# Linear attention plus mixture of experts on one core: six q tiles turned through DRAM instead of on TensorE, and the routing table's lanes as Sign steps on ScalarE

## The chip, the cores and the metric

The kernel runs on one core of a Trainium2 chip. The metric is the device time of one execution in microseconds (us); the time before is the median of three runs, 826.5 us (826.42 to 826.99). A profile of one execution goes with it. The engines are TensorE (PE in the profile; PEld is its weight load), VectorE (DVE), ScalarE (ACT), GpSimd (POOL) and SyncE (SP, which only issues transfers here). Each works its own instructions off in order and waits for the others through semaphores.

## The reference

```python
xn = _layernorm(x)                                   # (2048, 512)
# attention: 32 heads of 16, phi(t) = where(t > 0, t + 1, exp(t)) + 1e-6
q, k, v = split(xn @ wqkv)
pq, pk = phi(q), phi(k)
kv = einsum("bhsd,bhse->bhde", pk, v);  z = sum_s(pk)
num = einsum("bhqd,bhde->bhqe", pq, kv)
den = einsum("bhqd,bhd->bhq", pq, z)[..., None] + 1e-6
attn = (num / den).reshape(S, D) @ wo
# experts: 8 of them, the best 2 of each token, softmax over the two logits
h = silu(x @ w1[e]) @ w2[e];  moe = sum_e gate_e * h
out = x + attn(xn) + moe(xn)
```

The 2048 tokens stand in 16 tiles of 128 (t = 0 to 15), the 512 features in 4 chunks of 128.

## The kernel before

All matrix products are made as three products of a high part (rounded to fp32r) and a low part (what the rounding left): PASSES on L45. split_hi (L140) makes the high part on ScalarE, split_lo (L143) the low part on VectorE. In the profile both appear under L141 and L144, told apart by the tile's name.

The kernel has three stages. The first normalizes the tokens, computes k and the logits, and sums up the attention's matrix G (to about 100 us). The second, which the change touches, computes the queries' side for tiles 0 to 10 in full and for tiles 11 to 15 up to the normalized features, and along with it the routing of tokens to experts. The third (from about 194 us) runs the experts; it is more than three quarters of the time, and at its end the last five q tiles are multiplied.

The order of work on each engine is the order in which the program writes it (manual_schedule, L691). The second stage is the loop of L1531, t = 4 to 13. In a step t:

- o_out(t-4) (L1476): VectorE adds the product of tile t-4 to x, SP stores it.
- a piece of the routing (side, L685; the generators of L456 and L676): in steps 4 to 6 small VectorE operations, in steps 7 to 10 table(q) for q = 0 to 3 (L639), in step 11 table_end (L663). table(q) makes, on VectorE, one-hot rows of the lane (ohl, 128 x 1024) and of the block (mvb, 128 x 528, two operations) for four token tiles. table_mm(q) (L655), eight matmuls, sums them up into the table of which token stands at which place; table_end turns that into the gather and scatter indices gidx and sidx.
- q_den(t-1), and the first half of q_norm(t-1) (L1408, L1412): VectorE sums the heads of pz, adds 1e-6, takes the reciprocal.
- q_proj(t) (L1372): TensorE, 12 matmuls of 512 columns; behind it ScalarE's three operations of q_exp (L1382).
- the table_mm of the step before.
- the second half of q_norm(t-1): GpSimd multiplies with the reciprocal (L1416).
- q_feat(t) (L1399): VectorE q_phi (L1393), then GpSimd q_mult (L1397).
- load_x(t-2), and in steps up to 12 q_transp(t-2) (L1419): TensorE transposes pz of tile t-2, four matmuls of 128 columns into PSUM; ScalarE takes the high part, VectorE the low part of the result, pqT.
- plain_w (L944), in steps 11 to 13: the first expert's weights are split, ScalarE high, VectorE low.
- o_proj(t-3) (L1431): TensorE, 12 matmuls with pqT of tile t-3.

In steps 11 to 13 GpSimd gathers the first expert's token rows (gather1, L1042) with gidx, and x_block (L1087) transposes them on TensorE.

The late tiles 11 to 15 (NO = 11 onward) already go another way: pz_out (L1440) stores pz to DRAM, and near the end of the kernel pz_in (L1443) loads it back in 32-row blocks, four transfers each; q_turn (L1449) turns the 32 x 32 blocks on VectorE in two operations, and q_hi and q_lo (L1456, L1460) split the result.

Of the kernel before, what the change touches and what calls it, by code (L numbers as in the profile page):

```python
# [8 lines left out]
F32 = mybir.dt.float32  # L9
# [11 lines left out]
P = 128  # L21
# [24 lines left out]
ND = 5  # L46
NO = NT - ND
NE = 12
NP = NF // 2
# [36 lines left out]
def linear_attn_plus_moe(  # L86
# [24 lines left out]
    pz_d = tc.dram_tile((ND * P, D), F32, name="pz_d")  # L111
    xs_d = tc.dram_tile((E * RB * P, D), F32, name="xs_d")
    gate_d = tc.dram_tile((E, BLK, P), F32, name="gate_d")
    sx_d = tc.dram_tile((P, BLK), F32, name="sx_d")
# [111 lines left out]
    def constants_b():  # L226
        def iota(t, pattern, base=0, cm=0):
# [11 lines left out]
                        compare_op=ALU.is_ge, fill=0.0, base=DH - 1, channel_multiplier=-1)  # L239
        iota(i_lane, [[1, P]])  # L240
        iota(i_blk, [[1, NB]])
        iota(i_ov, [[1, NOV]])
# [200 lines left out]
    rt = cst  # L443
    lane_f = rt.tile([P, NT, 2], F16, name="lane_f")
    blk_f = rt.tile([P, NT, 2], F16, name="blk_f")
# [10 lines left out]
    def routing():  # L456
# [176 lines left out]
        V.tensor_scalar(la_i, sl_i, 7, None, op0=ALU.arith_shift_right)  # L633
        V.tensor_copy(blk_f, la_i)
        yield 3.0

    tabp = {}

    def table(q):  # L639
        ts = slice(4 * q, 4 * q + 4)  # L640
        ohl = ta(f"ohl{q}", 8 * P, F16).rearrange("p (a b) -> p a b", a=8)
        mvb = ta(f"mvb{q}", 8 * NB, F16).rearrange("p (a b) -> p a b", a=8)
        la = lane_f[:, ts, :].rearrange("p t k -> p (t k)").unsqueeze(2)
        bl = blk_f[:, ts, :].rearrange("p t k -> p (t k)").unsqueeze(2)
        V.tensor_tensor(ohl, i_lane.unsqueeze(1).broadcast_to([P, 8, P]),
                        la.broadcast_to([P, 8, P]), op=ALU.is_equal)
        V.tensor_tensor(mvb, i_blk.unsqueeze(1).broadcast_to([P, 8, NB]),
                        bl.broadcast_to([P, 8, NB]), op=ALU.is_equal)
        m4 = mvb.rearrange("p (t k) b -> p t (k b)", k=2)
        V.tensor_tensor(m4, m4, i_tok[:, ts].unsqueeze(2).broadcast_to([P, 4, 2 * NB]), op=ALU.mult)  # L650
        tabm[q] = (ohl, mvb)

    tabm = {}

    def table_mm(q):  # L655
# [3 lines left out]
        for i in range(8):  # L659
            T.matmul(tabp[0], ohl[:, i, :], mvb[:, i, :],  # L660
                     start=(q == 0 and i == 0), stop=(q == 3 and i == 7))

    def table_end():  # L663
        tab = wp.tile([P, 2, NB], F32, tag="tab", name="tab", bufs=1)
        t1, em = tab[:, 0, :], tab[:, 1, :]
# [701 lines left out]

    pq, pz, pqT = {}, {}, {}

# [35 lines left out]
    def heads(ap):  # L1405
        return ap.rearrange("p (h d) -> p h d", d=DH)
# [5 lines left out]
    def q_norm(t):  # L1412
        den = dens.pop(t)
        V.tensor_scalar(den, den, 1e-6, None, op0=ALU.add)
        V.reciprocal(den, den)
        G.tensor_tensor(heads(pz[t]), heads(pq[t]),  # L1416
                        den.unsqueeze(2).broadcast_to([P, H, DH]), op=ALU.mult)

# [12 lines left out]
    def o_proj(t):  # L1431
        tag = "acc" if t < NO else ("mm", "tr", "acc")[(t - NO) // 2]
        ops_[t] = [(psm(tag, f"op{t}_{c}", w), slice(o, o + w)) for c, (o, w) in enumerate(o_cols(t))]
        for op, cols in ops_[t]:
            for kc in range(KC):
                for i, (a, b) in enumerate(PASSES):
                    T.matmul(op, pqT[t][:, a, kc * P:(kc + 1) * P], M_v[kc // 2][b][:, kc % 2, cols],  # L1437
                             start=(kc == 0 and i == 0), stop=(kc == KC - 1 and i == 2))

    def pz_out(t):  # L1440
        Q.dma_start(pz_d[(t - NO) * P:(t - NO + 1) * P, :], pz.pop(t))

    def pz_in(t):  # L1443
        pz[t] = ta(f"pzr{t}")
        rows = pz_d[(t - NO) * P:(t - NO + 1) * P, :].rearrange("(c j) (a f) -> a j c f", j=BLK, f=P)
        for a in range(4):
            Q.dma_start(pz[t][a * BLK:(a + 1) * BLK].rearrange("j (c f) -> j c f", f=P), rows[a])

    def q_turn(t):  # L1449
        src = pz.pop(t).rearrange("p (c k i) -> p c k i", i=BLK, k=KC)  # L1450
        pz[t] = ta(f"pzt{t}")
        dst = pz[t].rearrange("p (k c j) -> p c k j", k=KC, j=BLK)
        for q in range(2):
            V.transpose(dst[:, :, 2 * q:2 * q + 2, :], src[:, :, 2 * q:2 * q + 2, :])

    def q_hi(t):  # L1456
        pqT[t] = tb(f"pqT{t}").rearrange("p (h c) -> p h c", h=2)
        split_hi(pqT[t][:, 0], pz[t])
# [70 lines left out]
    q_feat(3)  # L1529

    for t in range(OLAG + 1, NT - 2):  # L1531
        if t < NO + OLAG:
            o_out(t - OLAG - 1)
        due, late[:] = late[:], []
        spent = 0.0
        while spent < PERIOD:
# [3 lines left out]
            spent += c  # L1540
        q_den(t - 1)
        if 8 <= t < 11:
            fetch_w()
        q_proj(t)
        for f in due:
            f()
        if t in (11, 12):
            gather1(0, 2 * t - 22)
        if t == 12:
            x_block(0, 0)  # L1550
        if t == 13:
            gather1(0, 4)
        q_norm(t - 1)
        if t > NO:
            pz_out(t - 1)
# [224 lines left out]
```

## Time and profile before

| what | value |
|---|---|
| median of 3 runs | 826.5 us |
| the profiled execution, its own time | 826.48 us |
| span of the profile, first to last instruction | 824.8 us |
| mean granted TensorE clock | 1.000 |
| DMA, all queues | 127.69 MB, mean 155 GB/s |
| transposes of pz on TensorE (L1422) | 44 matmuls, 119.8 to 178.9 us |
| table matmuls (L660) | 32 matmuls, 153.0 to 169.3 us |

The page's columns: a group of instructions has its line, engine, operation, tiles and shapes, then busy time and mean duration. A row of the timeline has the start in the span, the duration, engine, line, operation and tiles, a count (x), and in brackets the idle time of the engine just before and what ended it. A row of a window has its length, the busy time of each engine, and then the granted clock, the DMA engines' busy share and GB/s. A matmul's duration includes its way through the array; the distance of two starts is what it costs in a stream.

### The profile page before, as it was taken

Reading aid. Unit: us, or ns where it says so; the run is one execution under the profiler, and the core shown is the slowest. Engines: PE = TensorE matmul, PEld = TensorE weight load, DVE = VectorE, ACT = ScalarE, POOL = GpSimd, SP = SyncE. Lnnn points to the kernel's source line nnn. Section 1 sums busy time; section 2 is a strip of 40 time slices with the busy share of each in tenths; the row PEclk is TensorE's granted clock in tenths of the full one; section 3 lists DMA queues with packets and bytes.
Section 4 is the critical chain, followed back from the end, with each engine's and each line's share of the span. In section 5 each row is a group of like instructions: output and inputs, shape, how many; then the busy total and the mean of one; then the engine's idle time right before and its main releaser. Section 6 shows DMA issues by size and latency. Waiting matters only on the chain. (4 is left out here: it accounts for less than half of the span.)

```text
span 824.8 us, 15897 instructions
## 1 busy us (share of the span) xinstructions
PE 820.3 (99%) x5361; PEld 752.1 (91%) x5361; DVE 679.6 (82%) x1470; ACT 541.2 (66%) x1162; POOL 249.7 (30%) x335
## 2 busy tenths in 40 slices
PE   9999999999999999999999999999999999999998
PEld 8999888889999999999999999999999888888886
DVE  7788889999878887878888788789888987887851
ACT  5575364358666768766876777677768766776650
POOL 5543224375310136121803250443127030012002
PEclk9999999999999999999999999999999999999999
DMA  5752136354764565566557464756576573249507
GB/s 168 252 199 87 52 135 202 128 183 166 234 200 135 152 197 108 145 166 184 131 136 187 151 143 136 206 130 161 155 190 130 161 188 113 84 132 232 154 1 178
DMA packets 106874, 127.69 MB, mean 155 GB/s; under 512 B 15198, under 2 KB 69854, under 8 KB 106758
## 3 DMA queue, kind: packets, MB, share of 16 engines
q1 hardware_dynamic: 92902, 106.43, 42.7%
q0 software_dynamic: 12880, 18.66, 11.8%
q10 hardware_dynamic: 1008, 1.57, 0.5%
q8 instruction: 43, 0.70, 0.3%
q14 instruction: 41, 0.34, 0.1%
HBM read 93.95 MB, written 31.09 MB: 152 GB/s over the span
## 5 line engine op out<-in xcount | busy, mean ns | idle before, releaser
L1174 POOL DMA_INDIRECT out_dram<-yo,sidx x22 | 35.1, 1595 | 282.6 <-DVE yo L1169 260.4
L1174 POOL DMA_INDIRECT out_dram<-yu,L x47 | 78.0, 1659 | 85.9 <-ACT yu L1267 59.0
L144 DVE TENSOR_TENSOR h<-hs,h 128x576 fp32r<-128x576 f32 (+7 forms) x112 | 77.7, 694 | 5.7 <-ACT h L141 5.4
L141 ACT ACTIVATE h<-hs 128x576 fp32r<-128x576 f32 (+7 forms) x112 | 72.3, 646 | 3.2
L1324 ACT ACTIVATE hs<-px 128x276 f32<-128x276 f32 (+7 forms) x54 | 21.1, 390 | 58.7 <-PE px L1316 58.6
L1339 ACT ACTIVATE hs<-hs 128x276 f32<-128x276 f32 (+7 forms) x54 | 23.0, 426 | 46.5 <-DVE hs L1338 46.5
L1338 DVE TENSOR_TENSOR hs<-pz,hs 128x276 f32<-128x276 f32 (+7 forms) x54 | 23.3, 431 | 34.6 <-PE pz L1316 34.0
L1343 DVE TENSOR_TENSOR hs<-px,hs 128x276 f32<-128x276 f32 (+7 forms) x54 | 23.3, 432 | 33.7 <-PE px L1316 33.7
L1047 POOL DMA_INDIRECT xg<-xn_d,gidx x37 | 40.8, 1104 | 28.2 <-DMA xq<-xs_d 7.2
L437 PE MATMUL gacc<-pkhl,xnhl 128*128 128x512 f32 x192 | 47.9, 397 | 0.0
L437 PEld LDWEIGHTS gacc<-pkhl,xnhl 128*128 128x128 f32 x192 | 34.8, 188 | 6.8
L1173 POOL MEMSET spacer<- 1x1 f32 x69 | 38.4, 557 | 6.8 <-DVE ws_3l L144 6.8
L1349 DVE TENSOR_TENSOR hs<-py,hs 128x276 f32<-128x276 f32 (+7 forms) x54 | 23.0, 426 | 13.7 <-PE py L1316 13.4
L1344 ACT ACTIVATE hs<-hs 128x276 f32<-128x276 f32 (+7 forms) x54 | 22.8, 422 | 17.0 <-DVE hs L1343 15.8
L411 POOL TENSOR_TENSOR zz<-zz,pk 128x512 f32<-128x512 f32 x14 | 18.2, 1300 | 48.3 <-DVE L L404 48.3
L1385 ACT ACTIVATE e_q<-qp 128x512 f32<-128x512 f32 x16 | 9.6, 598 | 35.4 <-PE qp L1376 31.7
L1198 PE MATMUL y<-w_1h,h 128*128 128x512 f32 (+2 forms) x88 | 32.0, 394 | 0.0
L1198 PE MATMUL y<-w_5h,h 128*128 128x512 f32 (+2 forms) x88 | 32.0, 394 | 0.0
L1198 PE MATMUL y<-w_2h,h 128*128 128x512 f32 (+2 forms) x88 | 32.0, 393 | 0.0
L1198 PE MATMUL y<-w_3h,h 128*128 128x512 f32 (+2 forms) x88 | 32.0, 393 | 0.0
L1198 PE MATMUL y<-w_0h,h 128*128 128x512 f32 (+2 forms) x88 | 32.0, 393 | 0.0
L1198 PE MATMUL y<-w_4h,h 128*128 128x512 f32 (+2 forms) x88 | 31.7, 393 | 0.0
(563 smaller groups left out, 3152.8 us busy)
## 6 DMA issues: line engine op xcount, KB each, us to landing
wst<-in_B_w_dram SPq DMA_DIRECT2D x196, 128.0 KB
wst<-in_B_w_dram SPq DMA_DIRECT2D x37, 512.0 KB
zz<-in_B_w_dram SPq DMA_DIRECT2D x26, 512.0 KB
xs_d<-xg SPq DMA_DIRECT2D x117, 64.0 KB
xq<-xs_d SPq DMA_DIRECT2D x28, 256.0 KB
x<-in_A_x_dram SPq DMA_DIRECT2D x27, 256.0 KB
xn_d<-xn SPq DMA_DIRECT2D x16, 256.0 KB
xnT<-xn SPq DMA_DIRECT2D x11, 256.0 KB
```

The source lines that it names most:

```text
L141: A.activation(hi, src, AF.Copy)
L144: V.tensor_tensor(lo, src, raw(hi), op=ALU.subtract)
L437: T.matmul(gacc[d], xnhl[:, a, d * P:(d + 1) * P], pkhl[:, b, :], start=(t == 0 and i == 0), stop=(t == NT - 1 and i == 2))
L1047: G.indirect_dma_start(out=raw(t), out_offset=None, in_=xn_d, in_offset=IOA(ap=gidx[:, b:b + 1], axis=0))
L1173: G.memset(spacer, 0.0)
L1174: st = G.indirect_dma_start(out=rows, out_offset=IOA(ap=idx, axis=0), in_=src, in_offset=None, compute_op=ALU.add).ins
L1198: T.matmul(ya[r, d][:m], h[a][:, d * P:d * P + m], w[b][:, n % 2, :], start=(first and i == 0), stop=(last and i == 2))
L1338: V.tensor_tensor(c12, pz_, c12, op=ALU.add)
L1339: A.activation(c12, c12, AF.Silu)
L1343: V.tensor_tensor(c22, px, c22, op=ALU.add)
L1344: A.activation(c22, c22, AF.Silu)
L1349: V.tensor_tensor(c11, pz_, c11, op=ALU.add)
```

## The change

Tiles t = 4 to 9 (TURNED; counted from one, 5 to 10) take the late tiles' way, but within the loop: q_norm(t) writes its result with the features in another order, so that after the turn they stand as the transpose would have put them; pz_out(t) and pz_in(t) come in step t+1, q_turn(t) and q_hi(t) in step t+2 in the place of q_transp(t), q_lo(t) at the head of step t+3, behind o_out. o_proj(t) stays in step t+3.

The lanes of the table are no longer one-hot rows made on VectorE: for each of the eight columns of a table ScalarE computes Sign(lane - (i + 0.5)) over the 128 places i, four of them behind q_exp and four behind q_hi, in steps 6 to 9, one step before the rest of the table. The table matmuls then give sums of steps; table_split takes high and low part of them at the head of step 11, and table_diff multiplies by a matrix of +-0.5 (made by table_steps on GpSimd in step 8), which takes differences of neighbouring rows and so gives the table. table_end and q_den(10) come behind it in step 11. x_block(0, 0) moves in step 12 from ahead of the transposes to behind o_proj.

```diff
+TURNED = range(4, NO - 1)
+    pq_d = tc.dram_tile((len(TURNED) * P, D), F32, name="pq_d")
+        G.tensor_scalar(i_lane, i_lane, 0.5, None, op0=ALU.add)
-    lane_f = rt.tile([P, NT, 2], F16, name="lane_f")
+    lane_f = rt.tile([P, NT, 2], F32, name="lane_f")
...
+        lanes.append(0)
         yield 3.0
+    lanes = []
+    def table_lanes(h):
+        if not lanes or lanes[0] == 4:
+            return
+        q = lanes[0]
+        if h == 0:
+            tabm[q] = raw(um(f"ohl{q}"))[:, :4 * P].bitcast(F16).rearrange("p (a b) -> p a b", a=8)
+        la = lane_f[:, 4 * q:4 * q + 4, :].rearrange("p t k -> p (t k)")
+        for i in range(4 * h, 4 * h + 4):
+            A.activation(tabm[q][:, i, :], i_lane, AF.Sign, bias=la[:, i:i + 1], scale=-1.0)
+        lanes[0] += h
     def table(q):
-        ohl = ta(f"ohl{q}", 8 * P, F16).rearrange("p (a b) -> p a b", a=8)
-        V.tensor_tensor(ohl, i_lane.unsqueeze(1).broadcast_to([P, 8, P]),
-                        la.broadcast_to([P, 8, P]), op=ALU.is_equal)
...
+    def table_steps():
+        step, tabp[2] = ta("step", P), um("step_r")[:, :P]
+        G.memset(step, 0.0)
+        for base, v in ((0, -0.5), (-1, 0.5), (P - 1, -0.5)):
+            G.affine_select(out=step, in_=step, pattern=[[1, P]], compare_op=ALU.not_equal,
+                            fill=v, base=base, channel_multiplier=-1)
+        G.tensor_copy(tabp[2], step)
+    def table_split():
+        tab = wp.tile([P, 2, NB], F32, tag="tab", name="tab", bufs=1)
+        hl = um("tabhl")
+        tabp[1] = tab, hl[:, :NB], hl[:, NB:2 * NB]
+        split(*tabp[1][1:], tabp[0])
+    def table_diff():
+        for i in range(2):
+            T.matmul(tabp[0], tabp[2], tabp[1][1 + i], start=(i == 0), stop=(i == 1))
...
+            if q == 1:
+                table_steps()
             late.append(lambda q=q: table_mm(q))
             yield 9.0
-        table_end()
...
+        out, src, den = heads(pz[t]), heads(pq[t]), den.unsqueeze(2).broadcast_to([P, H, DH])
+        if t in TURNED:
+            out = pz[t].rearrange("p (a k h d) -> p k a h d", a=4, k=KC, d=DH)
+            src, den = (ap.rearrange("p (k a h) d -> p k a h d", a=4, k=KC) for ap in (src, den))
+        G.tensor_tensor(out, src, den, op=ALU.mult)
...
     def pz_in(t):
-        pz[t] = ta(f"pzr{t}")
+        if t in TURNED:
+            both = raw(tb(f"pzr{t}"))
+            pz[t], pzt[t] = both[:, :D], both[:, D:]
+        else:
+            pz[t] = ta(f"pzr{t}")
...
     for t in range(OLAG + 1, NT - 2):
+        diff = done == [table_mm]
+        if diff:
+            table_split()
+            done.append(table_split)
         if t < NO + OLAG:
             o_out(t - OLAG - 1)
+        if t - 3 in TURNED:
+            q_lo(t - 3)
...
-        q_den(t - 1)
+        if not diff:
+            q_den(t - 1)
...
         q_proj(t)
+        table_lanes(0)
         for f in due:
             f()
+        if diff:
+            table_diff()
+            table_end()
+            q_den(t - 1)
...
-        if t == 12:
-            x_block(0, 0)
...
         q_norm(t - 1)
-        if t > NO:
+        if t > NO or t - 1 in TURNED:
             pz_out(t - 1)
         q_feat(t)
...
             load_x(t - 2)
-            q_transp(t - 2)
+            if t - 1 in TURNED:
+                pz_in(t - 1)
+            if t - 2 in TURNED:
+                q_turn(t - 2)
+                q_hi(t - 2)
+            else:
+                q_transp(t - 2)
+        table_lanes(1)
         if t >= 11:
             plain_w()
         if t - OLAG < NO - 1:
             o_proj(t - OLAG)
-        while 3 in tabm:
+        while 3 in tabm and type(tabm[3]) is tuple:
             late.pop(0)()
+            if 3 not in tabm:
+                done.append(table_mm)
+        if t == 12:
+            x_block(0, 0)
```

More of the change, by code (lines that the diff above doesn't have):

```diff
@@ L634, in routing @@
         V.tensor_copy(blk_f, la_i)
+        lanes.append(0)
         yield 3.0
     tabp = {}
+    lanes = []
[9 more added lines that the diff above has]
+        lanes[0] += h
     def table(q):
         ts = slice(4 * q, 4 * q + 4)
-        ohl = ta(f"ohl{q}", 8 * P, F16).rearrange("p (a b) -> p a b", a=8)
         mvb = ta(f"mvb{q}", 8 * NB, F16).rearrange("p (a b) -> p a b", a=8)
-        la = lane_f[:, ts, :].rearrange("p t k -> p (t k)").unsqueeze(2)
         bl = blk_f[:, ts, :].rearrange("p t k -> p (t k)").unsqueeze(2)
-        V.tensor_tensor(ohl, i_lane.unsqueeze(1).broadcast_to([P, 8, P]),
-                        la.broadcast_to([P, 8, P]), op=ALU.is_equal)
         V.tensor_tensor(mvb, i_blk.unsqueeze(1).broadcast_to([P, 8, NB]),
@@ L650, in table @@
         V.tensor_tensor(m4, m4, i_tok[:, ts].unsqueeze(2).broadcast_to([P, 4, 2 * NB]), op=ALU.mult)
-        tabm[q] = (ohl, mvb)
+        tabm[q] = (tabm[q], mvb)
     tabm = {}
+    def table_steps():
[5 more added lines that the diff above has]
+        G.tensor_copy(tabp[2], step)
     def table_mm(q):
@@ L661, in table_mm @@
                      start=(q == 0 and i == 0), stop=(q == 3 and i == 7))
+    def table_split():
[6 more added lines that the diff above has]
+            T.matmul(tabp[0], tabp[2], tabp[1][1 + i], start=(i == 0), stop=(i == 1))
     def table_end():
-        tab = wp.tile([P, 2, NB], F32, tag="tab", name="tab", bufs=1)
+        tab = tabp[1][0]
         t1, em = tab[:, 0, :], tab[:, 1, :]
@@ L1366, in linear_attn_plus_moe @@
                     zt.unsqueeze(1).broadcast_to([P, n, D]))
-    pq, pz, pqT = {}, {}, {}
+    pq, pz, pzt, pqT = {}, {}, {}, {}
     eq = {}
@@ L1415, in q_norm @@
         V.reciprocal(den, den)
-        G.tensor_tensor(heads(pz[t]), heads(pq[t]),
-                        den.unsqueeze(2).broadcast_to([P, H, DH]), op=ALU.mult)
+        out, src, den = heads(pz[t]), heads(pq[t]), den.unsqueeze(2).broadcast_to([P, H, DH])
[3 more added lines that the diff above has]
+        G.tensor_tensor(out, src, den, op=ALU.mult)
     def q_transp(t):
@@ L1438, in o_proj, with rows_d @@
                              start=(kc == 0 and i == 0), stop=(kc == KC - 1 and i == 2))
+    def rows_d(t):
+        return pq_d[(t - TURNED[0]) * P:(t - TURNED[0] + 1) * P, :] if t in TURNED else \
+            pz_d[(t - NO) * P:(t - NO + 1) * P, :]
     def pz_out(t):
-        Q.dma_start(pz_d[(t - NO) * P:(t - NO + 1) * P, :], pz.pop(t))
+        Q.dma_start(rows_d(t), pz.pop(t))
     def pz_in(t):
-        pz[t] = ta(f"pzr{t}")
-        rows = pz_d[(t - NO) * P:(t - NO + 1) * P, :].rearrange("(c j) (a f) -> a j c f", j=BLK, f=P)
+        if t in TURNED:
[3 more added lines that the diff above has]
+            pz[t] = ta(f"pzr{t}")
+        rows = rows_d(t).rearrange("(c j) (a f) -> a j c f", j=BLK, f=P)
         for a in range(4):
@@ L1450, in q_turn @@
         src = pz.pop(t).rearrange("p (c k i) -> p c k i", i=BLK, k=KC)
-        pz[t] = ta(f"pzt{t}")
+        pz[t] = pzt.pop(t) if t in TURNED else ta(f"pzt{t}")
         dst = pz[t].rearrange("p (k c j) -> p c k j", k=KC, j=BLK)
@@ L1456, in q_hi @@
     def q_hi(t):
-        pqT[t] = tb(f"pqT{t}").rearrange("p (h c) -> p h c", h=2)
+        pqT[t] = (sm if t in TURNED else tb)(f"pqT{t}").rearrange("p (h c) -> p h c", h=2)
         split_hi(pqT[t][:, 0], pz[t])
@@ L1529, in linear_attn_plus_moe @@
     q_feat(3)
+    done = []
     for t in range(OLAG + 1, NT - 2):
+        diff = done == [table_mm]
+        if diff:
+            table_split()
+            done.append(table_split)
         if t < NO + OLAG:
             o_out(t - OLAG - 1)
+        if t - 3 in TURNED:
+            q_lo(t - 3)
         due, late[:] = late[:], []
```

## The prediction

> **What bounds the kernel now.** I read the page from the top, then the timeline of each engine between 118 and 195 us, where the q tiles are, and the waits of that stretch. The page's first part says which engine sets the end; the first row of the second fence is from the waits.
>
> ```profile
> PE 820.3 (99%) x5361; PEld 752.1 (91%) x5361; DVE 679.6 (82%) x1470; ACT 541.2 (66%) x1162; POOL 249.7 (30%) x335
> ```
>
> ```profile
> ACT e_q L1385 <- PE qp L1376: 28.7, 10, 4.1
> ```
>
> TensorE is busy 99% of the span, so any time that it works less, or waits more, shows one for one in the end. ScalarE waits about 2.9 us per step here for TensorE: it has room. How close VectorE follows is seen only in the timelines. TensorE first (start, duration, line):
>
> ```profile
> 134.86 0.40 PE L1376 MATMUL qp<-wq1h,xnT 128*128 128x512 f32 x1
> 135.09 0.60 PE L1422 MATMUL pqp<-ident_r,pz 128*128 128x128 f32 x4
> ...
> 135.76 0.39 PE L1437 MATMUL op<-M0l,pqT 128*128 128x512 f32 x1
> ...
> 138.28 0.39 PE L1376 MATMUL qp<-wq0h,xnT 128*128 128x512 f32 x1
> ...
> 144.30 0.39 PE L1376 MATMUL qp<-wq0h,xnT 128*128 128x512 f32 x1
> ...
> 147.38 0.48 PE L1437 MATMUL op<-M0h,pqT 128*128 128x512 f32 x1
> ...
> 150.23 0.39 PE L1376 MATMUL qp<-wq0h,xnT 128*128 128x512 f32 x1
> ...
> 168.86 0.43 PE L660 MATMUL tabp<-mvb,ohl 128*128 128x66 f16 x8
> 169.13 0.48 PE L1376 MATMUL qp<-wq0h,xnT 128*128 128x512 f32 x1
> ...
> 175.19 0.39 PE L1376 MATMUL qp<-wq0h,xnT 128*128 128x512 f32 x1
> ...
> 178.60 0.47 PE L1437 MATMUL op<-M0h,pqT 128*128 128x512 f32 x1
> ...
> 181.43 0.39 PE L1376 MATMUL qp<-wq0h,xnT 128*128 128x512 f32 x1
> ```
>
> The rows at 138.28, 144.30, 150.23, 169.13, 175.19 and 181.43 are the starts of steps t = 6, 7, 8, 11, 12 and 13. A 512-wide matmul costs 0.227 us from start to start (134.86 to 135.09), so the 12 of q_proj and the 12 of o_proj cost 2.72 us each. Four transposes hold TensorE from 135.09 until the second matmul behind them starts at 135.76: 0.67 less 0.227, so **0.44 us**. Eight table matmuls cost 0.27 us (168.86 to 169.13). Now VectorE:
>
> ```profile
> 144.34 0.68 DVE L1410 TENSOR_REDUCE den<-pz 128x32 f32<-128x512 f32 x1
> ...
> 145.54 0.63 DVE L1393 SCALAR_TENSOR_TENSOR pq<-qp,e_q 128x512 f32<-128x512 f32 x1
> 146.09 0.68 DVE L144 TENSOR_TENSOR pqT<-pqp,pqT 128x512 fp32r<-128x512 f32 x1
> 146.68 0.68 DVE L1478 TENSOR_TENSOR x<-op,x 128x512 f32<-128x512 f32 x1
> 147.28 1.88 DVE L645 TENSOR_TENSOR ohl<-i_lane,lane_f 128x1024 f16<-128x1024 f16 x1
> 149.08 0.70 DVE L647 TENSOR_TENSOR mvb<-i_blk,blk_f 128x528 f16<-128x528 f16 x1
> ...
> 150.44 0.68 DVE L1410 TENSOR_REDUCE den<-pz 128x32 f32<-128x512 f32 x1
> ```
>
> No row has an idle time in brackets: VectorE runs without a gap, one operation behind the other, and lags TensorE. The sum o_out(3) of step 7 starts at 146.68 although its matmuls ended near 144.3. So here two engines are full, and what is put on VectorE ahead of something that TensorE needs is paid. From start to start: the denominator chain 1.20 (144.34 to 145.54), q_phi 0.55, low part 0.59, o_out 0.60, the is_equal that makes the lanes 1.80 (147.28 to 149.08), the rest of a table 1.36 (149.08 to 150.44).
>
> **The change, part by part.** *Removed from TensorE:* six times four transposes, 6 x 0.44 = 2.64 us, in steps 6 to 11. That is all it can save there. *Removed from VectorE:* four is_equal of 1.80 us in steps 7 to 10, and the low part of step t is put at the head of step t+1. *Added:* for the round trip and the turn, these rows, the late tiles' own and a store and load of the same size:
>
> ```profile
> 145.77 1.06 POOL L1416 TENSOR_TENSOR pz<-pq,den 128x512 f32<-128x512 f32 x1 [3.55 <-DVE den L1415]
> ```
>
> ```profile
> 147.39 0.33 SPq L1480 DMA_DIRECT2D out_dram<-x  x1
> ...
> 768.64 1.85 SPq L1447 DMA_DIRECT2D pzr<-pz_d  x4
> ```
>
> ```profile
> 149.20:150.20 1.00, 1.00 (x6) 0.83 (x5) 0.97 (x2) 0.53 (x2) 0.00 (x0) 1.00 0.67 227
> 771.20:771.60 0.40, 0.40 (x6) 0.40 (x5) 0.31 (x1) 0.18 (x1) 0.00 (x0) 1.00 0.50 147
> ```
>
> ```profile
> 756.17 0.76 DVE L1454 STREAM_TRANSPOSE pzt<-pzr 128x256 f32<-128x256 f32 x2
> L141 ACT ACTIVATE pqT<-pzt x5: 615/624/639, 772.2 to 795.7; 128x512 fp32r<-128x512 f32 x5
> L144 DVE TENSOR_TENSOR pqT<-pzt,pqT x5: 682/686/692, 773.0 to 796.6; 128x512 fp32r<-128x512 f32 x5
> ```
>
> In the window rows the last three numbers are the granted clock, the DMA engines' share and GB/s. Store: a 256 KB store issued at 147.39 and a load behind it both move until about 150.2 (DMA share 0.67 in the first window row); the store alone, as the first half, I estimate at 2.0 us to its landing, between 1.8 and 2.8. Load: the four issues begin at 768.64, their bytes still move in 771.20 to 771.60: 3.1 us. **Round trip 5.1 us, between 4.9 and 6.1**; the four loads wait on SP for the store's landing, and the loads of x and, in steps 8 to 10, a 512 KB weight block stand ahead in the same queue, which can add 1 us. The multiplication on GpSimd (1.06 us) now writes in a permuted order that no row shows: 1.06 at best, 1.3 if it behaves like the kernel's other full-tile products; 1.1 taken. Turn 0.76, high part 0.62 plus 0.07 to be seen, low part 0.69.
>
> *Signs:* the nearest row is four 128 x 128 activations with a per-partition scale:
>
> ```profile
> 313.27 1.26 ACT L1267 ACTIVATE yu<-yu,gu 128x128 f32<-128x128 f32 x4
> ```
>
> So 2 x 1.26 us per step on ScalarE in steps 6 to 9. It fits the 2.9 us of room; if that cover were gone, the next exponentials would be late, and up to 1.26 us of it would come before q_phi. The step matrix on GpSimd (five small operations in step 8, in its 3.55 us of idle time) and the 0.5 added to the lanes at the start cost nothing that TensorE waits for. *table_diff:* two narrow matmuls, between 0.07 (two of the eight above) and 0.22 (half of four transposes); 0.15 taken.
>
> *Where TensorE now waits.* Step 6 loses its transposes: step 7 starts at 138.28 + 5.44 = 143.7 and wants o_proj(4) at 146.4. But tile 4 is turned only when VectorE's full queue reaches it: q_phi(6) ends at 146.09 as before (nothing ahead of it is removed), the round trip of a product that ended near 141.0 arrives at 146.1 to 146.3, the turn ends at 147.0, o_out(3) at 147.6, the high part at 147.7, the low part at 148.4. o_proj(4) starts at **148.5**, against 147.38 before; step 8 at 151.2, against 150.23: **1.0 us later**.
>
> Steps 8 to 10 win back. TensorE needs 5.44 + 0.27 = 5.71. The loop through the other engines takes two steps: denominator 1.20, product 1.25 with its waits, trip 5.1, turn 0.76, high 0.7, low 0.7, table 1.36: 11.1, or 5.5 a step, up to 6.0 with the weights in the way. Before, steps 8 to 11 took 169.13 - 150.23 = 18.90; now 3 x 5.71 + 0.27 = 17.4 to about 18.2. Step 11 starts between 0.5 us earlier and 0.3 later.
>
> Step 11 and 12 give it away again. Rows of before:
>
> ```profile
> 171.63 0.22 DVE L666 COPY tab<-tabp 128x66 f32<-128x66 f32 x1
> ...
> 172.88 0.68 DVE L1410 TENSOR_REDUCE den<-pz 128x32 f32<-128x512 f32 x1
> ...
> 174.84 0.68 DVE L144 TENSOR_TENSOR pqT<-pqp,pqT 128x512 fp32r<-128x512 f32 x1
> 175.67 2.43 DVE L144 TENSOR_TENSOR w_0l<-wst,w_0h 128x1024 fp32r<-128x1024 f32 x1
> ...
> 182.16 1.48 DVE L144 TENSOR_TENSOR w_1l<-wst,w_1h 128x1024 fp32r<-128x1024 f32 x1 [0.26 <-ACT w_1h L141]
> ```
>
> ```profile
> 174.58 1.05 ACT L141 ACTIVATE w_0h<-wst 128x1024 fp32r<-128x1024 f32 x1
> ```
>
> The low part of tile 9 was done at 175.52, **ahead of** the weight split w_0l, 3.1 us before o_proj(9) at 178.60. q_lo(9) now stands at the head of step 12, **behind** w_0l. VectorE from the low part of tile 8 on: table_end 1.25, denominator 1.20, q_phi 0.55, turn 0.76; then ScalarE's high part and w_0h, 0.69 + 0.98, as w_0l waits for them; w_0l 1.4 (between 1.4 and 2.4 by the two rows), o_out 0.60, low part 0.69 and 0.07: 8.2 us from low part to o_proj(9). TensorE needs from o_proj(8) to o_proj(9) 2.72 + 2.72 + 0.44 = 5.9, and then stands for **2.3 us**, a little less where o_proj(8) itself starts late by TensorE's own work.
>
> **The sum.** Step 13, before at 181.43: step 12 starts 0.7 earlier to 0.5 later (step 11's shift, 0.15 for table_diff, 0.44 for the transposes gone, up to 0.6 wait of o_proj(8) behind the table's split); the wait adds 2.3 to 2.6; x_block stays 0.37, only moved behind o_proj. That is +1.8 to +2.8, and I take **+2.3 us**. Behind it TensorE is full, so nothing gives it back. The profiled execution took 826.48 us (span 824.8 and 1.7 around it), as good as the median 826.5: **828.8 us**. A weight split of 2.4 us or trips of 6 us would make 830.5.
>
> One rule speaks against the change. The Trainium skill, "VectorE: DVE Perf Modes", section "Rules for kernel authors", says to do a 128 x 128 transpose on TensorE if PSUM is a fit destination. By that rule the exchange would cost more than the 2.64 us that it frees; the trace agrees in part, since the transposes cost 0.44 us on the full engine and their replacement 0.76 on another full one.
>
> **Rivals.** *TensorE alone decides* (faster): were the low parts in time, as ScalarE's room and the lighter VectorE of steps 7 to 10 argue, TensorE would save 2.64 and pay 0.15: 824.0. Against it stands the gapless queue at 144 to 147. Chance 0.09. *Only one wait stays* (no change): step 7 loses 1.0, steps 8 to 11 win it back, and the wait in step 12 is under 1 us because VectorE arrives earlier than I have it: 825.5 to 827.5, near 826.5. Chance 0.24. *Sign needs another table set than the exponential.* Table loads stand in the trace twice, one of them
>
> ```profile
> L1296 ACT ACT_TABLE_LOAD x1 | 1.3, 1283 | 0.0
> ```
>
> at 1.28 us, before the first Silu. Two a step would raise ScalarE's step from 2.5 + 2.5 to 7.6 us against TensorE's 5.7: 4 x 1.9 = 7.6 more, 836. It decides if such loads appear between Exp and Sign. The Trainium skill, "ScalarE: Activation LUTs", section "Table sets: the hidden batching unit", names relu, copy, identity and abs as filler of every set, and leaves Sign out there; no run here shows it yet. Chance 0.03. *The clock drops in a wait*: it is granted at 1.00 in every window row above. If a wait put it to half for the next q_proj, that costs 2.7 more, 831.5. The Trainium skill, "TensorE: Matmul & The Clock Gate", section "Why this matters for your kernels", warns of gaps over about 3 us; my waits are 2.1 and 2.3. Chance 0.04. *The forecast* has the remaining 0.60; its own range is 827.8 to 830.3, and 0.06 of it lies under 828.15.
>
> **How the numbers follow.** A measurement of this kernel can tell about 0.2% (1.65 us) from no change. Slower by more: 0.54 of the forecast, with 0.03 and 0.04: 0.61. Within: 0.24 + 0.06 = 0.30. Faster: 0.09. The range from 826.0 to 830.8 leaves out the fast rival, the table loads, the clock, and the tail of the others: about 2 in 10.
>
> **What would show it.** TensorE's timeline: gaps of about 2 us ahead of o_proj in step 7 and in step 12 (released by pqT's low part on L144), none over 0.7 between. VectorE: idle before the turn in step 9 or 10 if the trips are late; w_0l between the turn and the low part of tile 9. ScalarE: four Signs in about 1.2 us, and no table load. Wrong would be: o_proj(9) without a wait, low parts that come before TensorE asks, or a wait at a place that I don't name (GpSimd's permuted product above 2 us, the gathers behind the later table).

## The result, and the profile after
The changed kernel takes 838.54 us (median of 4 runs, 838.19 to 839.31) against 826.75 for the kernel before in the same session (4 runs): a ratio of 1.0143, 95% interval 1.0126 to 1.0161. It is slower, as forecast, but by 11.8 us and not by 2.3. (Of the last run below, with the turns in mixed order, two of six executions took 996.2 and 1342.6 us at a mean granted clock of 0.75 and 0.56, and its median is that of the other four.) The profiled execution has a span of 836.9 us, 12.1 more than before. On the page of after, engine by engine:

```profile
PE 822.3 (98%) x5339; PEld 750.8 (90%) x5339; DVE 676.6 (81%) x1479; ACT 550.9 (66%) x1195; POOL 253.4 (30%) x341
```

TensorE has 22 instructions less: 24 transposes gone, two matmuls of table_diff added. (Its busy time rose by 2 us all the same, because some matmuls ran at half clock; see below.) The time went into waits. TensorE's timeline of after, the first matmul of each step that matters and each wait (idle time in brackets, and who ended it):

```profile
143.72 0.39 PE L1408 MATMUL qp<-wq0h,xnT 128*128 128x512 f32 x1
...
147.84 0.50 PE L1472 MATMUL op<-M0h,pqT 128*128 128x512 f32 x1 [1.24 <-ACT pqT L143]
...
151.09 0.39 PE L1408 MATMUL qp<-wq0h,xnT 128*128 128x512 f32 x1
...
156.96 0.39 PE L1408 MATMUL qp<-wq0h,xnT 128*128 128x512 f32 x1
...
162.81 0.39 PE L1408 MATMUL qp<-wq0h,xnT 128*128 128x512 f32 x1
...
168.10 0.52 PE L1472 MATMUL op<-M0h,pqT 128*128 128x512 f32 x1 [2.14 <-ACT pqT L143]
...
172.89 0.48 PE L1408 MATMUL qp<-wq0h,xnT 128*128 128x512 f32 x1
...
176.32 0.38 PE L692 MATMUL tabp<-tabhl,step_r 128*128 128x66 f32 x2 [0.43 <-DVE tabhl L146]
...
184.85 0.50 PE L1472 MATMUL op<-M0h,pqT 128*128 128x512 f32 x1 [1.72 <-ACT pqT L143]
...
188.26 0.74 PE L1472 MATMUL op<-M0h,pqT 128*128 128x512 f32 x2 [2.68 <-DVE pqT L146]
...
192.55 0.46 PE L1408 MATMUL qp<-wq0h,xnT 128*128 128x512 f32 x1
```

The steps' starts, beside those of before (same line of q_proj in each trace):

| start of step | 7 | 8 | 9 | 10 | 11 | 12 | 13 | 15 |
|---|---|---|---|---|---|---|---|---|
| before | 144.30 | 150.23 | 156.45 | 162.65 | 169.13 | 175.19 | 181.43 | 187.51 |
| after | 143.72 | 151.09 | 156.96 | 162.81 | 172.89 | 179.81 | 192.55 | 198.71 |
| difference | -0.58 | +0.86 | +0.51 | +0.16 | +3.76 | +4.62 | +11.12 | +11.20 |

Up to step 10 it goes as forecast. Then step 10 loses 3.6 us, step 11 0.9 and step 12 6.5. The expert stage keeps the distance, and the last 0.9 us come at its end (last section). Two things make up the loss. The first is in SyncE's queue (start, how long the issuing took, transfer). L1480 is a tile's store, L1490 its four loads, L965 and L971 weight blocks:

```profile
152.43 0.34 SPq L1480 DMA_DIRECT2D pq_d<-pz  x1
152.81 0.42 SPq L157 DMA_DIRECT2D x<-in_A_x_dram  x1
154.49 1.74 SPq L1490 DMA_DIRECT2D pzr<-pq_d  x4
156.33 0.38 SPq L1523 DMA_DIRECT2D out_dram<-x  x1
157.81 0.43 SPq L965 DMA_DIRECT2D wst<-in_B_w_dram  x1
158.33 0.47 SPq L1480 DMA_DIRECT2D pq_d<-pz  x1
158.89 0.38 SPq L157 DMA_DIRECT2D x<-in_A_x_dram  x1
162.77 2.25 SPq L1490 DMA_DIRECT2D pzr<-pq_d  x4
165.11 0.38 SPq L1523 DMA_DIRECT2D out_dram<-x  x1
165.69 0.41 SPq L965 DMA_DIRECT2D wst<-in_B_w_dram  x1
166.14 0.56 SPq L1480 DMA_DIRECT2D pq_d<-pz  x1
...
173.67 0.50 SPq L1480 DMA_DIRECT2D pq_d<-pz  x1
...
178.99 1.76 SPq L1490 DMA_DIRECT2D pzr<-pq_d  x4
```

and in what VectorE does with the loads, the turns of tiles 6 to 9:

```profile
157.89 0.77 DVE L1497 STREAM_TRANSPOSE pzr<-pzr 128x256 f32<-128x256 f32 x2 [0.18 <-DMA pzr<-pq_d]
...
166.61 0.77 DVE L1497 STREAM_TRANSPOSE pzr<-pzr 128x256 f32<-128x256 f32 x2 [3.39 <-DMA pzr<-pq_d]
...
174.37 0.77 DVE L1497 STREAM_TRANSPOSE pzr<-pzr 128x256 f32<-128x256 f32 x2 [2.49 <-DMA pzr<-pq_d]
...
183.37 0.77 DVE L1497 STREAM_TRANSPOSE pzr<-pzr 128x256 f32<-128x256 f32 x2 [3.14 <-DMA pzr<-pq_d]
```

Call a trip the time from a tile's store to its turn. Tile 6: 152.43 to 157.89, 5.46 us, and its loads could be issued 2.06 us behind the store. Tile 7, whose store stands 0.5 us behind a weight block: loads 4.44 us behind the store, trip 8.28 us. The next tile is hit twice: its product on GpSimd ended at 163.88, but SyncE was still at the loads of tile 7 and then issued another block, so the store left at 166.14. Trip 8.23; that of tile 9, 173.67 to 183.37, is 9.70, and its loads went 5.32 us behind the store.

The second is the clock. Windows of half a microsecond of after; the number behind the POOL column is the granted clock:

```profile
168.00:168.50 0.50, 0.40 (x2) 0.30 (x2) 0.42 (x1) 0.50 (x3) 0.00 (x0) 0.94 0.68 166
169.00:169.50 0.50, 0.50 (x3) 0.40 (x3) 0.47 (x2) 0.50 (x2) 0.00 (x0) 0.50 1.12 401
171.50:172.00 0.50, 0.50 (x3) 0.40 (x2) 0.37 (x1) 0.00 (x0) 0.50 (x1) 0.65 0.19 58
188.50:189.00 0.50, 0.50 (x3) 0.40 (x3) 0.47 (x2) 0.50 (x1) 0.00 (x0) 0.92 0.43 66
192.00:192.50 0.50, 0.50 (x5) 0.32 (x3) 0.50 (x1) 0.00 (x0) 0.50 (x1) 0.67 0.84 230
```

A mean of 0.94 between 1.00 and 0.50 puts the switch at 168.44, 0.65 puts the return at 171.85: 3.41 us at half clock, and again from 188.92 to 192.33. Each costs about half its length, 1.7 us: o_proj(7) takes 4.5 us (168.10 to 172.63), o_proj(6) took 2.9. Before, the clock was 1.00 throughout.

### The profile page after: what moved, and what is told of

It reads as the page before. It is cut to its first block, busy times and chain, and to the rows that moved or that the text cites. A ratio compares the mean times of both kernels' runs of the same rounds, so it can differ in the third digit from the quotient of the medians.

```text
span 836.9 us, 15952 instructions
## 1 busy us (share of the span) xinstructions
PE 822.3 (98%) x5339; PEld 750.8 (90%) x5339; DVE 676.6 (81%) x1479; ACT 550.9 (66%) x1195; POOL 253.4 (30%) x341
## 5 line engine op out<-in xcount | busy, mean ns | idle before, releaser
L1452 POOL TENSOR_TENSOR pz<-pq,den 128x512 f32<-128x512 f32 x16 | 17.6, 1099 | 49.6 <-DVE den L1447 49.6
```

## The experiments
All times are medians, each ratio stands to the kernel before in the same session. The theories: A, the weight blocks make the trips late; B, a trip through DRAM is too slow here anyway; C, the lanes cost the time; D, the low part of tile 9 waits behind w_0l; E, the half clock is a cost of its own.

### One part of the change alone
The lanes without the turn (TURNED empty), and the turn without the lanes (is_equal on VectorE and table_end as before the change):

```diff
-TURNED = range(4, NO - 1)
+TURNED = ()
...
```

> The lanes, the step matrix, the split and the moved end of the table as after the change; all tiles turned on TensorE as before it. Theories A, B and D (the turn costs it all): 826.5 to 828 us, near the kernel before (826.75), with clock 1.00 in all of the stretch from 140 to 200 us. Theory C (the lanes cost the time): 832 us or more, with a gap ahead of table_diff or ahead of a q_proj that waits for ScalarE.

> The turn of tiles 4 to 9 through DRAM as after the change; the lanes as is_equal on VectorE and the end of the table as before it. Theories A, B and D: 836 us or more, all of the loss; if VectorE's lanes (about 1.2 us in each of four steps) then stand ahead of the turns, up to 4 us above the changed kernel. Theory C: below 830 us.

Lanes only: 826.67 us, ratio 0.9997 (95% interval 0.9987 to 1.0006), no wait of TensorE above 0.15 us from 140 to 208 us, clock 1.00 there. Turn only: 839.04, ratio 1.0138 (1.0121 to 1.0155). C falls: alone, the lanes cost and bring nothing, and the turn alone costs the whole.

### Which tiles
One run takes the first three tiles, the other range(7, 10):

```diff
-TURNED = range(4, NO - 1)
+TURNED = range(4, 7)
```

> Only tiles 4 to 6 are turned through DRAM, 7 to 9 on TensorE as before; lanes as changed. Theory A (weight blocks of steps 8 to 10 spoil the trips, the trip itself is good enough): the trips of tiles 4 to 6 take 5.2 to 5.6 us as in the changed kernel, o_proj(4) waits 1.2 us, and q_proj(10) starts near 162.8, where it does before (162.65): 825.5 to 827.5 us, so next to none of the loss of 12 us. Theory B (each trip costs alike, about 2 us a tile): 831 to 833 us.

> The complement: only tiles 7 to 9 are turned through DRAM. Theory A: trips of 8 us and more for them, all waits of steps 10 to 12 and both stretches of half clock as in the changed kernel: 836 to 839.5 us. Theory B: 831 to 833 us.

Tiles 4 to 6: 828.23 us, ratio 1.0017 (1.0007 to 1.0027), 0.7 us above A's range; o_proj(4) waits 1.31 us, nothing else does. Tiles 7 to 9: 836.47, ratio 1.0116, with waits of 2.28 us (table_diff) and 2.67 us (o_proj(9)). So the first three tiles cost 1.4 us and the other three 9.6. B falls, at least as "each trip alike".

### The weight block behind the turn
```diff
-        if 8 <= t < 11:
-            fetch_w()
         q_proj(t)
...
         table_lanes(1)
+        if 8 <= t < 11:
+            fetch_w()
```

> Only the issue of the weight block in steps 8 to 10 moves, from ahead of q_proj to behind the turn, so that the store and the four loads of a tile stand ahead of it in SyncE's queue. Theory A (the block is what makes the trips of tiles 7 to 9 take 8.3 to 10.5 us in place of 5.3 to 5.5): VectorE's waits of 3.39, 2.49 and 3.14 us ahead of the turns go below 0.7, the wait of o_proj(7) and with it the first stretch of half clock goes (that is 2.14 + 1.7 us), q_proj(11) starts near 169.3 instead of 172.9, and the 4.4 us that the first half of step 12 lost are in part kept, by the low part of tile 9: 831 to 834 us in place of 838.5. Theory B (going through DRAM is too slow here whatever stands in the queue): trips stay above 7 us and the time within 1.5 us of 838.5. Theory C (the lanes cost the time, not the turn): no change.

839.09 us: no gain, as B had it. SyncE's queue in that run says why the time is no test of A:

```profile
160.69 3.05 SPq L1490 DMA_DIRECT2D pzr<-pq_d  x4
164.82 0.43 SPq L965 DMA_DIRECT2D wst<-in_B_w_dram  x1
165.35 0.45 SPq L1523 DMA_DIRECT2D out_dram<-x  x1
165.85 0.42 SPq L1480 DMA_DIRECT2D pq_d<-pz  x1
166.33 0.47 SPq L157 DMA_DIRECT2D x<-in_A_x_dram  x1
170.37 1.74 SPq L1490 DMA_DIRECT2D pzr<-pq_d  x4
```

The first block now leaves behind tile 7's loads, and for that tile A held: its trip is 6.68 us (158.66 to 165.34) instead of 8.28, o_proj(7) waits 0.52 us instead of 2.14, and step 11 starts at 170.22 instead of 172.89. But the same block left 1.03 us ahead of the store of tile 8, whose loads could go only 4.52 us behind that store; SyncE had been held by tile 7's loads. The next block did the same to tile 9. Their trips are 7.9 and 10.2 us, table_diff waits 2.44 us, o_proj(9) 2.53 and 2.42 us, 6.8 us of half clock follow, and the gain is lost. Moved by most of a step in the program, a block moved in the queue only from one tile's store to the next tile's.

### The low part of tile 9 first
```diff
-        if t - 3 in TURNED:
+        if t - 3 in TURNED and t < 12:
             q_lo(t - 3)
...
+        if t == 11:
+            q_lo(9)
         if t >= 11:
             plain_w()
```

> Only the low part of tile 9 moves, from the head of step 12 to step 11, ahead of the first weight block's high and low part. Theory D (it waits behind w_0l on VectorE, as the forecast's step 12 had it): the 2.68 us wait inside o_proj(9) goes below 0.7, with it the second stretch of half clock, and q_proj(13) starts 3 to 4.5 us earlier: 834 to 835.5 us. If the late turn of tile 9 at 183.37 is the only cause, w_0l stands behind the turn in both orders, the wait of o_proj(9) shrinks by the 2.7 us and nothing else: the same figure; if neither, 838.5.

835.45 us, ratio 1.0101 (1.0084 to 1.0118): 3.1 us won, and no wait of o_proj(9) above 0.15 us is left. The expectation gave the same figure to a late turn as the only cause, so the time doesn't decide; the next runs do: with tile 9's turn 4.7 us earlier (178.68, next section) its low part is still 1.42 us late. D holds for that part. Another stretch of half clock, 176.8 to 180.3, came behind table_diff, which now waits 1.75 us.

### The block from ScalarE's queue
Only the issuing engine of the first three blocks changes:

```diff
+        L = A if i < 3 else Q
...
-                Q.dma_start(st, w1[ds(e, 1), :, cols]...
+                L.dma_start(st, w1[ds(e, 1), :, cols]...
...
```

> The three weight blocks of steps 8 to 10 are issued by ScalarE into its own DMA queue, at the same place of the step, so they no longer stand ahead of the store in SyncE's queue, and share the 16 DMA engines with it only. Theory A1 (it is the order in SyncE's queue): store to landing near 2.1 us, trips of 5.3 to 6.5 us, the wait of o_proj(7) below 0.7 and no half clock in step 10; the low part of tile 9 still waits behind w_0l: 830 to 833 us. Theory A2 (it is the sharing of the DMA engines, 512 KB at 3 us): trips still above 7.5 us and the time above 836.

832.99 us, ratio 1.0074 (1.0054 to 1.0094), inside A1's range: 5.6 us won, and the clock stays at 1.00 from 140 to 208 us. SyncE's queue, and one block in ScalarE's (ACTq):

```profile
158.65 0.34 SPq L1481 DMA_DIRECT2D pq_d<-pz  x1
...
160.74 1.74 SPq L1491 DMA_DIRECT2D pzr<-pq_d  x4
160.85 0.41 ACTq L966 DMA_DIRECT2D wst<-in_B_w_dram  x1
...
165.83 0.34 SPq L1481 DMA_DIRECT2D pq_d<-pz  x1
...
168.08 1.74 SPq L1491 DMA_DIRECT2D pzr<-pq_d  x4
```

The loads go 2.0 to 2.3 us behind the store again. But each block now leaves together with a tile's four loads (160.85 beside 160.74). The trips of tiles 6, 7 and 8, which have a block there, are 7.4, 8.2 and 7.1 us, where A1 had 6.5 at most, and VectorE waits 1.86 us for tile 6, which no block touched before; tile 9 has none beside its loads, and 5.8 us. So a block beside the loads costs 1.6 to 2.8 us, and A2 is true in part. As no block leaves close ahead of a store here, the run doesn't tell whether the store was held before by the order in SyncE's queue or by the block moving beside it. What it wins is short waits: 0.94 us at o_proj(6), 0.74 at o_proj(7), 1.42 for the low part of tile 9.

### A block ahead of tiles 4 to 6
The run with tiles 4 to 6 alone, with the suspected cost added where there was none:

```diff
+        if 5 <= t < 8:
+            st = stage(f"extra{t}").rearrange("p (k f) -> p k f", k=KC)
+            Q.dma_start(st, w1[0:1, :, :FG].rearrange("a (k p) f -> p (a k) f", p=P))
         q_proj(t)
```

> The run with tiles 4 to 6 alone (828.2 us), and in steps 5, 6 and 7 a 512 KB load of the same shape as the weight block into a stage tile that nothing reads, at the block's place ahead of q_proj, so ahead of the tile's store in SyncE's queue. Theory A: it makes the trips of tiles 4 to 6 what those of 7 to 9 are: 8 us and more in place of 5.2 to 5.6, VectorE's waits of 2 to 3.4 us ahead of the turns, a time of 832 to 837 us. Rival F (tiles 7 to 9 are slow because of what else runs in steps 8 to 12, the weight halves and the table, not because of the block): trips below 6.5 us and 828 to 829.5 us.

832.46 us, 4.2 more than without the loads.

```profile
137.59 0.43 SPq L1597 DMA_DIRECT2D extra<-in_B_w_dram  x1
...
140.93 0.33 SPq L1480 DMA_DIRECT2D pq_d<-pz  x1
...
145.23 0.44 SPq L1597 DMA_DIRECT2D extra<-in_B_w_dram  x1
146.78 0.33 SPq L1480 DMA_DIRECT2D pq_d<-pz  x1
```

The trips of tiles 5 and 6 become 8.0 and 9.2 us (146.78 to 154.79, 154.10 to 163.30), with VectorE's waits of 3.15 and 3.25 us ahead of the turn; o_proj(5) waits 2.14 us, and a stretch of half clock follows. This makes A the cause, and the rival F falls. But tile 4, which had a block ahead of it as well, is not late (trip 5.44 us): its block left 3.34 us ahead of its store, those of tiles 5 and 6 left 1.55 and 0.48 us ahead of theirs. So the block has to stand close. In the run with tiles 7 to 9 alone, tile 7 stands 3.0 us behind a block and lies between, with a trip of 6.7 us.

### No block in steps 8 to 10
The first lines of the edit, which take the three blocks from expert 0, are left out here:

```diff
...
-        if 8 <= t < 11:
+        for _ in range(3 if t == 4 else 0):
             fetch_w()
```

> The changed kernel, with the three weight blocks of steps 8 to 10 loaded in step 4, before any tile is stored; they come from expert 0, since the routing isn't known there, so the first expert's output is not the reference's, at the same work and traffic. Nothing of 512 KB is then in SyncE's queue while tiles 4 to 9 go through DRAM. Theory A (the blocks make the trips of tiles 7 to 9 late): all trips 5.2 to 5.8 us, VectorE waits below 0.8 us ahead of each turn, no half clock in step 10; what stays is the 1.2 us wait of step 7 and the low part of tile 9 behind w_0l: 828.5 to 831.5 us. Rival H (the place in the kernel, with what else runs there, makes them late): trips above 7 us and 834 or more.

> As the run without blocks in steps 8 to 10 (first weight blocks from expert 0, so another output for the first expert), and the low part of tile 9 ahead of the first weight halves in step 11. If late trips and this low part were all of it: 826 to 828 us, with only the 1.2 us wait of step 7 left, and a step of 5.8 us where TensorE alone sets it (6.2 before). If a gather is late next, as in the run with ScalarE's queue and the low part together: up to 830.

831.19 us, ratio 1.0056 (1.0042 to 1.0071), inside A's range: 7.4 us won. Trips of tiles 7 to 9: 6.6, 6.2, 5.5 us; clock 1.00 in the profiled execution. The two longest miss A's 5.8; tile 7's four loads took 2.98 us to issue, and what held them isn't settled; tile 8's turn waited for VectorE's own work. What is left is the wait of step 7, 2.07 us here, and that for the low part of tile 9, 1.86 us. The first is longer than the 1.24 us of the changed kernel because of this edit: the load of x that VectorE's addition of step 6 needs now stands behind the three blocks in SyncE's queue, and VectorE waits for it,

```profile
142.72 0.69 DVE L1522 TENSOR_TENSOR x<-op,x 128x512 f32<-128x512 f32 x1 [1.43 <-DMA x<-in_A_x_dram]
```

so that the turn of tile 4 comes later behind its other work.

With q_lo(9) early as well, by the edit shown above: 833.45 us, not 826 to 828 and not below 830. From step 8 to step 13 there is no wait (159.47 to 165.32 is a step of 5.85 us), and step 13 starts 2.0 us later than before. But the wait of step 7 was 2.32 us in that run (VectorE waited 1.63 us for x), and a half-clock stretch followed; and behind step 15 the first expert's x_block waits 2.36 us, with another half-clock stretch behind that.

### Block and low part together
The edits of the run with ScalarE's queue and of the one with the low part first, in one kernel:

```diff
+        L = A if i < 3 else Q
...
+        if t == 11:
+            q_lo(9)
...
```

> The block from ScalarE's queue and the low part of tile 9 ahead of the first weight block's halves, both together. The block's queue alone gave 833.0; in it o_proj(9) still waits 1.42 us for its low part. If the two causes add up: 831.3 to 831.8 us. If the low part was late only because the turn of tile 9 was late (it is 4.7 us earlier there): 833.

835.25 us, so neither: worse than the queue alone (two executions each, 834.58 and 835.91 against 832.97 and 833.00). Step 15 starts at 191.43, 1.0 us earlier than with the queue alone, and then

```profile
196.15 1.27 PE L1126 MATMUL xep<-ident_r,xg 128*128 128x128 f32 x8 [1.75 <-DMA xg<-xn_d,gidx]
```

TensorE waits for a gather, and 3.4 us at half clock follow. The gathers start from the table: at 173.40 before the change, at 177.26 here. This is the next thing that is late.

### Fillers in the waits
Eight filler matmuls ahead of o_proj(7), ten inside o_proj(9), into PSUM that nothing reads:

```diff
...
+        if t == 10:
+            warm(8, xT(t, 0, 0), wq_v[0][0][:, 0, :])
...
+                    if t == 9 and kc == 0 and i == 1:
+                        warm(10, pqT[t][:, 0, :P], M_v[0][0][:, 0, :])
```

> The changed kernel with filler matmuls into an unused PSUM tile: 8 (1.8 us) ahead of o_proj(7) in step 10, and 10 (2.3 us) behind the first two matmuls of o_proj(9) in step 12, both inside waits for other engines. Theory E (the two stretches of half clock, 3.41 us each with pitch 0.43 in place of 0.23, are a cost of the waits by themselves): the granted clock is 1.00 in both and the time 3 us lower, 835 to 836. Rival: the halved stretches are covered by the next wait, or come from the traffic and not from the idle TensorE: 838 to 839.

837.52 us, ratio 1.0129 (1.0109 to 1.0149), clock 1.00 in both places: 1.0 us won and not 3. Step 12 keeps its gain, o_proj(9) takes 2.7 us to the next step instead of 4.3. Step 10 gains 1.4 us (168.53 to 171.93 instead of 168.10 to 172.89) and gives it back: table_diff waits 2.01 us instead of 0.43, as the turn of tile 8 comes no earlier. So E is half right: the half clock goes, but only part of its price comes back.

### A step more for each tile
Loads at the head of the next step, turn and product one step later, and the low part of tile 9 ahead of the weight halves:

The edits of these three runs are shown in part; the addition to the output moves by a step too:

```diff
...
-        if t - 3 in TURNED:
-            q_lo(t - 3)
+        if t - 2 in TURNED:
+            pz_in(t - 2)
+        if t - 4 in TURNED and t < 13:
+            q_lo(t - 4)
...
-                q_turn(t - 2)
-                q_hi(t - 2)
+                q_turn(t - 3)
+                q_hi(t - 3)
...
-        if t - OLAG < NO - 1:
-            o_proj(t - OLAG)
+        if t < 7:
+            o_proj(t - 3)
+        elif t > 7:
+            o_proj(t - 4)
...
```

> Each turned tile gets a step more: its loads are issued at the head of the next step, ahead of the weight block, its turn and product come one step later (step 7 has no product, step 13 has that of tile 9, and the addition to the output is one step later too), and the low part of tile 9 stands ahead of the second weight block's halves. A trip then has 12 us where 8 to 10.5 were needed. If the loss was only the late trips: no wait of o_proj and no half clock, TensorE saves 6 x 0.44 and adds 0.22 for the table: 823.5 to 825.5 us against 826.7. Rival G (VectorE or ScalarE sets steps 7 and 13 as soon as the products move): 826.5 to 829 us, with waits of q_proj or o_proj for them there.

The next run, against this one, puts the turn first and the block last:

```diff
-        if t - 4 in TURNED and t < 13:
-            q_lo(t - 4)
+        if t - 3 in TURNED:
+            q_turn(t - 3)
+            q_hi(t - 3)
...
+        if t - 3 in TURNED:
+            q_lo(t - 3)
         if not diff:
             q_den(t - 1)
-        if 8 <= t < 11:
-            fetch_w()
...
+        if 8 <= t < 11:
+            fetch_w()
         table_lanes(1)
...
```

> As the run with a step more, with three orders changed: turn and high part of a tile stand at the head of its step (behind the addition to the output, ahead of the table's part) and its low part ahead of den, so no turn waits behind VectorE's 4 us of work left over from step 6, and no low part stands behind a weight half; the block of steps 8 to 10 is issued behind the tile's store and the load of x. If what was left of the loss in the run before (2.66 us of wait in step 8, 2.9 us of half clock, 1.31 us in step 12) was VectorE's order, all of it goes: q_proj(14) starts between 181.5 and 183, against 184.15 before the change, and the time is 823.5 to 826 us, the first that shows the 6 x 0.44 us of TensorE. If VectorE or a gather is late next: 826 to 829 us with a wait of o_proj for pqT or of xep for xg.

The third does that for tiles 4 to 6 only, and leaves the block where it was:

```diff
+        if t - 3 in range(4, 7):
+            q_turn(t - 3)
+            q_hi(t - 3)
...
+                if t - 3 >= 7:
+                    q_turn(t - 3)
+                    q_hi(t - 3)
...
+        if t in (11, 12):
+            q_lo(t - 3)
         table_lanes(1)
```

> A step more for each tile as in the two runs before; turn, high and low part of tiles 4 to 6 at the head of their step, those of 7 to 9 at its end, their low parts ahead of the weight halves, the weight block back ahead of q_proj and behind the loads. In the last run steps 7 to 9 had no wait and step 9 took 5.82 us, and its 4.71 us wait came from the turn of tile 7 at the head of step 10, 3.38 us ahead of its data; at the end of step 10 that data is in. If so: no wait above 0.8 us in steps 7 to 12, q_proj(11) near 164.8 and q_proj(14) between 181.5 and 183.5 (184.15 before the change), 823.5 to 826.5 us. If VectorE, which by then runs a step behind TensorE, sets the pace: waits for mvb or tabhl in steps 10 and 11 and 826.5 to 830 us.

One step later: 832.78 us, ratio 1.0075 (1.0061 to 1.0088). No turn waits for its loads, but step 7 without a product is short, so TensorE reaches o_proj(4) while VectorE still works at step 7. The turn comes at 150.70, behind its other work, and then

```profile
152.17 0.79 PE L1472 MATMUL op<-M0h,pqT 128*128 128x512 f32 x1 [2.66 <-ACT pqT L143]
```

with half clock from 151.8 to 158.6. That is what rival G named, VectorE late where the products move (it had steps 7 and 13), though the time lies above G's 829. Turn first: 831.97 us, ratio 1.0068 (1.0055 to 1.0082). Steps 7 to 9 run with one wait of 0.16 us, and step 9 shows the saving on TensorE:

```profile
153.05 0.39 PE L1408 MATMUL qp<-wq0h,xnT 128*128 128x512 f32 x1
...
158.87 0.39 PE L1408 MATMUL qp<-wq0h,xnT 128*128 128x512 f32 x1
...
169.57 0.60 PE L681 MATMUL tabp<-mvb,ohl 128*128 128x66 f16 x8 [4.71 <-DVE mvb L663]
```

5.82 us against 6.20 before. Then the turn of tile 7 stands at the head of VectorE's step 10, waits 3.38 us for loads that now stand behind the block, and holds up the table and all behind it. Mixed: 832.2 us, ratio 1.0076 (1.0062 to 1.0091). The turns of tiles 7 and 8 no longer wait, but in step 10 VectorE's addition waits 1.59 us for x, whose load stands behind the block in the same queue, and table_mm 2.27 us for VectorE. All three lie above the ranges expected of them, and with single executions between 831.6 and 834.7 us they can't be told from each other. None of the versions beats the kernel before; the lanes alone equal it.

## Why the prediction was wrong, point by point
- **The step that failed** is the round trip: "5.1 us, between 4.9 and 6.1", with the weight block that "can add 1 us". Without a block it held, 5.3 to 5.5 us for tiles 4 to 6. With one close ahead of the store it was 8.2 to 9.7 us, 2.7 us and more longer: the loads could go only 4.4 to 5.3 us behind the store instead of 2.1, and as they wait for that store at the head of SyncE's queue, the next store is late too, tile 8's by 2.26 us. The forecast priced the block at 1 us, for which it showed no row, and put what stands behind a waiting issue at nothing. With the blocks taken out, 7.4 of the 11.8 us are gone; with blocks put close ahead of tiles 5 and 6, these are late. Whether the store waits its turn behind the block or moves slower beside it, no run separates; the run with ScalarE's queue has the blocks beside the loads, where they cost 1.6 to 2.8 us.
- **"Steps 8 to 10 win back"** was right for steps 8 and 9 and wrong for step 10, where the forecast named no wait over 0.7 us and o_proj(7) waits 2.14. The saving on TensorE isn't a constant 0.44 us a tile: step 6 takes 5.44 us after and 6.02 before, 0.58 less, step 9 5.85 and 6.20, 0.35 less.
- **Step 7** was right: o_proj(4) at 147.84 (148.5 forecast), step 8 at 151.09 (151.2). The way there differs a little: the first matmul waits for the high part only, the third, at 148.68, for the low part. This wait is most of what the run with tiles 4 to 6 loses (828.2 us).
- **Step 12** was right in mechanism: the low part of tile 9 does wait behind w_0l, 2.68 us by the trace (2.3 forecast), as the two rows of VectorE below this item show. It is not alone: 1.72 us of wait for the late turn stand ahead of it, and 1.7 us of half clock behind it.

```profile
185.78 1.23 DVE L146 TENSOR_TENSOR w_0l<-wst,w_0h 128x1024 fp32r<-128x1024 f32 x1 [1.65 <-ACT w_0h L143]
...
187.53 0.68 DVE L146 TENSOR_TENSOR pqT<-pzr,pqT 128x512 fp32r<-128x512 f32 x1
```

- **The clock** had a chance of 0.04, because the waits would be shorter than 3 us. It was wrong to rest on that, as waits of 2.14 and 2.68 us were enough: the half clock came twice, 1.7 us each. The fillers show that it isn't additive, as 1.4 us of it lay over a wait that comes anyway.
- **The lanes** were right: four Signs take 1.26 us, the profile of after has the same two table loads as before, and the lanes alone change nothing. Sign costs no table load beside the exponential here.
- **GpSimd's permuted product** takes 1.06 us, as before, so nothing came of that. The rule cited from the Trainium skill, "VectorE: DVE Perf Modes", section "Rules for kernel authors", to transpose on TensorE, fits the result; the turn itself, 0.77 us on VectorE, was the small part of the price, and the way through DRAM the large one.
- The sum: 0.9 us by step 8, 0.7 won back, 3.6 in step 10, 0.9 in step 11, 6.5 in step 12, 0.9 behind: 12.1. The forecast had the first, the second, and 2.3 of the 6.5. Its own range was drawn too narrow as well: the terms it lists for step 13 add up to between +1.5 and +3.2 us, not +1.8 to +2.8; the middle is the same.

What stays open: whether a block ahead of a store is dear by the order in the queue or by moving beside it; how far ahead of a store it may stand; what held SyncE for 3 us in four issues. The wait of step 7 is 1.2 to 1.4 us in every run that keeps o_proj(4) there, but for the two with the blocks moved to step 4, whose 2.07 and 2.32 us come from that. Smaller blocks, and a third queue for the tile, were not tried.

## What to carry to other kernels
Before a transfer is put on a path that decides, write out its queue in the order in which the transfers can leave: a load of 512 KB issued 0.5 us ahead of a 256 KB store delayed the loads that waited for that store by 2.4 us, one issued 3.3 us ahead delayed nothing, and an issue that waited held everything behind it in its queue. Count slack on the engine that runs last: a step more in the program was no step more while VectorE lagged TensorE. And where a change adds a wait of TensorE, price the half clock behind it, but look whether the next wait covers it.

## What the runs showed of the hardware that was not expected
From 140 to 210 us every stretch of half clock in the kept traces lasts 3.4 us or twice that. In after the two start at 168.44 and 188.92, 20.48 us apart, which is six times 3.41; in the three other traces with two stretches the distances are 10.24 us (tiles 7 to 9), 17.06 (turn only) and 44.37 (no blocks, low part early), which is three, five and thirteen times 3.41. The Trainium skill, "TensorE: Matmul & The Clock Gate", section "Part 1: The HAM clock gate", says that activity is judged in free-running windows of 3413 ns; the trace agrees with that length and that grid. It says that an idle window brings the half clock. Here a partly idle one was enough: it followed waits of 2.14 and 2.68 us, and in the run with a gather late one of 1.75 us; it did not follow 2.07 us in the run without blocks. Where the wait falls in the grid explains most of this. Cut into stretches of 3.41 us from their own switches, the eleven traces with a half clock show (with TensorE's busy time as the profile has it): of the stretches at full clock, all 11 that were busy for less than 43% were followed by half clock, none that was busy for 58% or more, and four of the six between. The way back asks for more: the five stretches at half clock that were busy for 29 to 89% were followed by another, all 15 busy for 95% or more by full clock. This is read from traces made for other questions, and no run was made to test it.

The last 0.9 us of the loss come at the conditional loop behind the experts (L1770), in TensorE's own sequencer:

```profile
825.00 0.47 PE L1472 MATMUL op<-Mr0h,pqT 128*128 128x512 f32 x1 [0.96 <-PEq L1770]
```

The trace of before lists no idle time at that place; other runs list none, or between 0.21 and 0.94 us, so differences of under 1 us between two runs can come from there. Nothing of the change stands near it, and its cause was not looked for.
